# Reads as plain float32 products, and products of zeros where the planner expects TensorE to wait

## The chip, the cores and the metric

The program runs on one core of a Trainium2 chip, in one launch. The metric is the device time of that launch in microseconds (us). The profile names five engines: PE is TensorE (PEld its weight loads), DVE is VectorE, ACT is ScalarE, POOL is GpSimd, and SP issues most transfers.

## What is computed

Three stages follow each other; the second needs all rows of the first, since its rows are sorted by expert.

```python
def _attn_ref(x, state):                     # x 8x8x512x64, state 8x8x32x64
    scores = scale * np.matmul(x, state.transpose(0, 1, 3, 2))
    a = softmax(scores)                      # over the 32 states
    xread = np.matmul(a, state)
    scores2 = scale * np.matmul(state, x.transpose(0, 1, 3, 2))
    a2 = softmax(scores2)                    # over the 512 tokens
    sread = np.matmul(a2, x)
    return np.concatenate([xread, sread], axis=2)

def _moe_ref(x, expert_emb, tau, w1, w2):    # 4352 rows of 512, 8 experts
    expert_idx = np.argmax(xn @ en.T / tau, axis=1)
    out[mask] = gate_w[mask, None] * (np.maximum(x[mask] @ w1[e], 0.0) @ w2[e])

def _moe2_ref(x, w_in, w_out):               # 512 to 2048 to 512
    h = x @ w_in
    return (h * np.clip(h + 3.0, 0.0, 6.0) / 6.0) @ w_out
```

(`softmax` stands for the lines with max, exp and sum; the reads of the title are `xread`.)

## The kernel before

**Stages.** The attention works batch by batch (eight batches of 544 rows). `o_X` transposes the tokens on PE, `o_sc` forms the scores, `o_scs` to `o_nm` make the two softmaxes on DVE, ACT and POOL, `o_aT` transposes the weights of the first one back, and `o_xr` multiplies them by the states: four reads `xr` a batch, each of two halves. The states stand in a masked form, `sd`, which POOL makes for each batch (`o_sd`), with eight more columns that give the router's logits. `o_xrc` copies the read out of PSUM and `o_xd` stores it in DRAM (`xd`). In the last two batches the logits are taken by `o_lg` on DVE. Then `o_top`, `o_scan`, `o_rk`, `o_rank`, `o_bt`, `o_at`, `o_pg` and `o_gidx` sort the rows by expert: `rk` and `pg` are short products on PE, and `gidx` holds the row numbers that POOL gathers by.

**Float32 in two parts.** A product with an operand of type float32r is done from parts: the rounded value and what is left of it (`ah`, `al`; `sdh`, `sdl`; `wh`, `wl`), as high by high, high by low and low by high. ACT or DVE makes the high part, DVE or POOL the low part. The attention's transposes and scores are plain float32 products instead, without parts.

**The expert layer.** The first five slots of 128 rows belong to the largest expert (the lead: `QUAD` of four slots and `FIFTH`); POOL gathers them into `xg`, ACT or DVE reorders them (`xp`), PE transposes them (`m_g`), and `L1w`/`L1` and `L2` form `h_g` and `y_g`. After the lead come eleven pairs of slots and ten single slots (`h_ps`, `y_ps`). Four further single slots stand in nested conditions at the program's end, which the run of the profile does not enter. Weights come in 512 KB loads (`raw`), of which two buffers exist; `load_w` makes `wh` and `wl`.

**The feed-forward layer** works on blocks of 256 rows: `F1` (tile `u_ps`, 12 products for each of 16 pieces) and `F2` (tile `o`, 6 products). Its weights are stored in a packed form, and `convert` unpacks each of the 32 pieces in eight steps on ACT, DVE and POOL (`cv_raw`, `cv_m`, `wih`, `wil`, `woh`, `wol`); eight of these fall into the attention. `F1` and `F2` stand between the pairs and singles.

**What sets the order.** Each engine works through its instructions strictly in the order in which they are written. That order comes from a planner (`Sched`): every step has a priority, an engine or a choice of engines (`"*"` in `BY`), and an assumed cost. `run` takes the step that can begin soonest, weighed with its priority, and advances the assumed clocks. PSUM and SBUF buffers are rings that a step takes and gives. So a changed cost can move steps on every engine, up to the point where the orders agree again: on PE that is the region of the fourth pair (about 440 us in the trace); behind it PE's order is the old one.

`REST` and `COLD` let the planner charge a slow start after an idle time of PE. `o_warm` runs 14 products at the very beginning.

Of the kernel before, what the change touches and what calls it, by code (L numbers as in the profile page):

```python
# [8 lines left out]
F32 = mybir.dt.float32  # L9
# [29 lines left out]
class Sched:  # L39
# [60 lines left out]
    def run(self, until=None):  # L100
        while self.avail and not (until and until()):
# [53 lines left out]
def kernel(  # L155
# [60 lines left out]
    def quarters(t, g):  # L216
# [28 lines left out]

    NRAW, NW, NROW, NGX = 2, 3, 6, 4
# [3 lines left out]
        ps=4, ax=NAX, xT=NXT, scs=NSC, e2=NE2, e1=NE1, a2=NA2, ah=NAH, al=NAH, xr=NXR, sd=2, sx=1, xs=1, acr=2,  # L250
# [110 lines left out]
    def ps(name):  # L361
        return pa.tile([128, 2, 512], F32, tag="ps", name=name)
# [84 lines left out]
    gh_ = one.tile([128, B, 2, E], F32R, name="gh_")  # L447
    gl_ = one.tile([128, B, 2, E], F32R, name="gl_")
    sth = one.tile([128, B, 2, D], F32R, name="sth")
    stl = one.tile([128, B, 2, D], F32R, name="stl")  # L450
# [31 lines left out]
    def o_sth(b0, b1):  # L482
        ACT.copy(sth[:, b0:b1], st[:, b0:b1])

    def o_stl(b0, b1):
        bs = slice(b0, b1)
        DVE.tensor_tensor(stl[:, bs], st[:, bs], f32(sth[:, bs]), op=ALU.subtract)
# [32 lines left out]
    def o_warm():  # L520
        p = ps("warm")
        for _ in range(14):
            PE.matmul(p[:, 0, 0:128], ident, ident, start=True, stop=True)

    def o_sd(b):
        res = []
        for s_, g_, nm in ((sth, gh_, "sdh"), (stl, gl_, "sdl")):
            t = ap2.tile([128, 2, W // 2], F32R, tag=nm, name=nm)
            for g in range(2):
                v = t[:, g].rearrange("p (h q w) -> p h q w", h=2, q=2)  # L530
                for h in range(2):
                    POOL.tensor_tensor(
                        v[:, h, :, 0:64].rearrange("p q (i a) -> p q i a", i=2),
                        f32(s_[:, b, g, :]).rearrange("p (q a) -> p q a", q=2).unsqueeze(2).to_broadcast([128, 2, 2, 32]),
                        bmask.rearrange("p (i h) -> p h i", i=2)[:, h].unsqueeze(1).unsqueeze(3).to_broadcast([128, 2, 2, 32]),
                        op=ALU.mult)
            POOL.tensor_copy(t.rearrange("p g (q w) -> p g q w", q=4)[:, :, :, 64:66],
                             f32(g_[:, b]).rearrange("p g (q i) -> p g q i", q=4))
            res.append(t)
        V["sd", b] = res  # L540
# [124 lines left out]
    def o_ah(b, r0, r1):  # L665
        if r0 == 0:
            V["ah", b] = ap1.tile([128, 2, 512], F32R, tag="ah", name="ah", bufs=NAH)
        k = slice(r0 * 128, r1 * 128)
        ACT.copy(V["ah", b][:, :, k], V["aT", b, r0][:, :, k])

    def o_al(b, r0, r1):
        if r0 == 0:
            V["al", b] = ap1.tile([128, 2, 512], F32R, tag="al", name="al", bufs=NAH)
        k = slice(r0 * 128, r1 * 128)
        DVE.tensor_tensor(V["al", b][:, :, k], V.pop(("aT", b, r0))[:, :, k], f32(V["ah", b][:, :, k]), op=ALU.subtract)

    def parts(b):
        ah, al = V["ah", b], V["al", b]
        sh, sl = V["sd", b]
        return (ah, sh), (ah, sl), (al, sh)  # L680

    def o_xr(b, r):
# [82 lines left out]
    def group(b0, b1, prio):  # L765
# [11 lines left out]
        q2 = op(lambda: o_gp(b0, b1), {"D": 0.35}, prio + 2, [q1])  # L777
        s1 = op(lambda: o_sth(b0, b1), {"A": 0.22 + 0.13 * n}, prio + 2, [ld], (), [hst])
        s2 = op(lambda: o_stl(b0, b1), {"D": 0.06 + 0.14 * n}, prio + 2, [s1], (), [hst])
        for b in range(b0, b1):  # L780
            st_ready[b], g_ready[b] = c, [q2, s2]
# [12 lines left out]
        X0c='A', X1c='*', nm='P', a2c='A', x0c='*', x1c='*', x2c='A', x3c='*', q1='A')  # L794

    PARTS = [(0, R)], [(k, k + R // 2) for k in (0, R // 2)]
    def batch(b, t, last):
# [3 lines left out]
        bscs, be2, ba2, bah, bal, bxr, bsd = (hold(n) for n in ("scs", "e2", "a2", "ah", "al", "ax" if last else "xr", "sd"))  # L801
# [40 lines left out]
        sd = do("sd", o_sd, {"P": 3.2}, g_ready[b], [bsd], port="P")  # L842
        for (r0, r1), scs in zip(chunks, scs_):
# [1060 lines left out]
```

## Time and profile before

| what | us |
|---|---|
| median of 3 runs | 1457.59 (1456.26 to 1458.63) |
| the profiled execution, its own time | 1456.29 |
| its span in the trace | 1454.6 |
| PE busy, DVE busy | 1349.5, 917.5 |
| ACT busy, POOL busy | 598.0, 433.8 |

Busy times are sums of an engine's own instructions and overlap between engines. A matrix product is recorded from its start to its modelled end, some 0.17 us after the next can begin, so distances between starts tell what a product costs in a row of them. PEclk is the TensorE clock that was granted, as a share of 2.4 GHz; 0.5 is its lower level, 1.2 GHz. Row L1650 and the like are lines of the kernel before.

### The profile page before, as it was taken

The numbers are of one execution on the slowest core, as the hardware profiler recorded it, in microseconds if no ns is written. First come the engines' busy times: TensorE is split into PE (matmuls) and PEld (weight loads), VectorE is DVE, ScalarE is ACT, GpSimd is POOL, SyncE is SP. The second block draws the span as 40 slices with busy tenths as digits, with TensorE's granted clock in tenths as the row PEclk, the third lists the DMA queues.
The fourth block names the chain that finished last, engine by engine and source line by source line (L and its number), as shares of the span: only waits on it lengthen the run. The fifth ranks groups of instructions, "written<-read, shape, count | busy, mean of one in ns | idle before, by whom it ended". The sixth has DMA issues, their size and how long they took to land. (4 is left out here: it accounts for less than half of the span.)

```text
span 1454.6 us, 25083 instructions
## 1 busy us (share of the span) xinstructions
PE 1349.5 (93%) x8976; PEld 1195.2 (82%) x8976; DVE 917.5 (63%) x2108; ACT 598.0 (41%) x1290; POOL 433.8 (30%) x483
## 2 busy tenths in 40 slices
PE   7985698787789999999999999999999999999997
PEld 5765676677678898988899898998988999899996
DVE  6988777688766545655564645777867676434332
ACT  3775425455434333424333343343344444333332
POOL 5453427414143242325132133332423311100000
PEclk8998689898899999999999999999999999999999
DMA  6654326556465333334333232545554544101000
GB/s 160 169 168 141 121 70 179 156 172 190 136 190 168 95 103 105 111 92 120 119 97 114 91 117 88 173 145 159 172 153 145 163 151 141 57 23 30 16 15 15
DMA packets 151765, 175.63 MB, mean 121 GB/s; under 512 B 43785, under 2 KB 116489, under 8 KB 150609
## 3 DMA queue, kind: packets, MB, share of 16 engines
q1 hardware_dynamic: 128544, 121.19, 27.7%
q0 software_dynamic: 12336, 35.99, 8.1%
q10 hardware_dynamic: 10752, 16.78, 3.7%
q8 instruction: 73, 1.20, 0.4%
q14 instruction: 60, 0.48, 0.1%
HBM read 146.09 MB, written 27.82 MB: 120 GB/s over the span
## 5 line engine op out<-in xcount | busy, mean ns | idle before, releaser
L1650 PE MATMUL u_ps<-yh,wih 128*128 128x256 f32 x1088 | 306.5, 282 | 9.0 <-ACT yh L1626 8.1
L1650 PE MATMUL u_ps<-yw,wih 128*128 128x256 f32 x1088 | 306.5, 282 | 0.1
L1650 PE MATMUL u_ps<-yh,wil 128*128 128x256 f32 x1088 | 306.0, 281 | 0.0
L1654 ACT ACTIVATE r<-u_ps,three 128x256 f32<-128x256 f32 x272 | 129.2, 475 | 353.0 <-PE u_ps L1650 348.5
L1657 DVE SCALAR_TENSOR_TENSOR u_ps<-r,u_ps 128x256 f32<-128x256 f32 x272 | 116.4, 428 | 226.1 <-ACT r L1654 225.5
L1650 PEld LDWEIGHTS u_ps<-yh,wih 128*128 128x128 f32 x1088 | 206.7, 190 | 18.3 <-ACT yh L1626 8.3
L1685 PE MATMUL o<-woh,gh 128*128 128x512 f32 x544 | 217.0, 399 | 1.5 <-DVE yo L1699 1.2
L1685 PE MATMUL o<-wol,gh 128*128 128x512 f32 x544 | 216.1, 397 | 0.0
L1685 PE MATMUL o<-woh,gl 128*128 128x512 f32 x544 | 214.8, 395 | 0.0
L1650 PEld LDWEIGHTS u_ps<-yw,wih 128*128 128x128 f32 x1088 | 206.0, 189 | 8.5 <-DVE yw L1629 0.4
L1650 PEld LDWEIGHTS u_ps<-yh,wil 128*128 128x128 f32 x1088 | 206.6, 190 | 0.0
L1280 DVE TENSOR_TENSOR wl<-raw,wh 128x512 fp32r<-128x512 f32 x275 | 192.9, 711 | 11.3 <-ACT wh L1277 6.9
L1544 PE MATMUL y_ps<-wh,hx 128*128 128x512 f32 x512 | 185.7, 399 | 0.0
L1661 ACT CAST gh<-u_ps 128x256 fp32r<-128x256 f32 x272 | 101.4, 373 | 201.9 <-PE o L1685 162.3
L1664 DVE TENSOR_TENSOR gl<-u_ps,gh 128x256 fp32r<-128x256 f32 x272 | 114.8, 422 | 108.2 <-ACT gh L1661 107.6
L1280 POOL TENSOR_TENSOR wl<-raw,wh 128x512 fp32r<-128x512 f32 x77 | 105.3, 1368 | 245.9 <-DVE wh L1277 124.7
L1308 POOL DMA_INDIRECT xq<-xd,qidx x128 | 131.8, 1030 | 85.0 <-DVE xt L1361 34.1
L1441 PE MATMUL h_ps<-xt,wh 128*128 128x256 f32 x704 | 141.3, 290 | 1.4 <-DVE wh L1277 1.0
L1277 DVE CAST wh<-raw 128x512 fp32r<-128x512 f32 x223 | 96.4, 436 | 64.2 <-DMA raw<-in_moe_w_dram 29.4
L1704 POOL DMA_INDIRECT out_dram<-yo,ix x34 | 37.8, 1112 | 320.1 <-DVE yo L1699 219.1
L1685 PEld LDWEIGHTS o<-woh,gl 128*128 128x128 f32 x544 | 102.4, 188 | 25.1
L1441 PEld LDWEIGHTS h_ps<-xt,wh 128*128 128x128 f32 x704 | 118.1, 198 | 4.1 <-PE u_ps L1650 1.2
(307 smaller groups left out, 2342.3 us busy)
## 6 DMA issues: line engine op xcount, KB each, us to landing
raw<-in_moe_w_dram SPq DMA_DIRECT2D x176, 512.0 KB, 4.0
yl<-ysd SPq DMA_DIRECT2D x136, 64.0 KB, 2.4
xd<-xr SPq DMA_DIRECT2D x8, 1056.0 KB, 4.5
ysd<-yt POOLq DMA_DIRECT2D x32, 256.5 KB, 3.3
xb<-in_x_dram SPq DMA_DIRECT2D x48, 128.0 KB, 2.9
yw<-in_moe_w_out_dram ACTq DMA_DIRECT2D x9, 512.0 KB, 4.5
cv_raw<-in_moe_w_in_dram ACTq DMA_DIRECT2D x8, 512.0 KB, 4.6
yh<-in_moe_w_in_dram ACTq DMA_DIRECT2D x8, 512.0 KB, 4.6
```

The lines of the kernel that those rows point to most:

```text
L1277: copy[e](pc["hi"], box["t"][:, j, :])
L1280: eng[e].tensor_tensor(pc["lo"], box["t"][:, j, :], f32(pc["hi"]), op=ALU.subtract)
L1308: POOL.indirect_dma_start(q[:, j * QW:(j + 1) * QW], None, xd_q, index(qidx[:, j, s:s + 1]))
L1441: PE.matmul(out(f), pc[w][:, (2 * c + f) * 128:(2 * c + f + 1) * 128], u.xt[a][:, 2 * j + c, 256 * hf:256 * hf + 256], start=new and c == ...
L1544: PE.matmul(u.y[i], u.ht[t][:, a, lo + 128 * i:lo + 128 * i + 128], pc[w], start=c == 0 and k == 0, stop=c == KF - 1 and k == 2)
L1650: PE.matmul(p, w, y[:, k, :], start=k == 0 and j == 0, stop=k == KD - 1 and j == 2)
L1654: ACT.activation(q["r"], q["p"], AF.Relu, bias=pool["three"][:, 0:1])
L1657: DVE.scalar_tensor_tensor(q["p"], q["r"], 6.0, q["p"], op0=ALU.min, op1=ALU.mult)
L1661: ACT.copy(q["h"], q["p"])
L1664: DVE.tensor_tensor(q["l"], q["p"], f32(q["h"]), op=ALU.subtract)
L1685: PE.matmul(o["o"][a], g[:, a * 128:(a + 1) * 128], w, start=m == 0 and j == 0, stop=m == KFF - 1 and j == 2)
L1704: POOL.indirect_dma_start(out, bass.IndirectOffsetOnAxis(ap=o["ix"][:, a:a + 1], axis=0), box["t"], None)
```

## The change

It has two parts.

**Reads as plain float32 products.** The parts of the read go: `o_gp`, `o_stl`, `o_al` and the second half of `o_sd` (the tile `sdl`) are dropped, `ah`, `sd` and the copied state `stk` are plain float32, and a read takes two products of 264 columns where it took six. The copy `ah` may now go to ACT or to DVE (the planner puts the last half batch's second half on DVE, all others on ACT), the read's assumed cost goes from 0.66 to 0.9, that of `o_sd` from 3.2 to 1.65.

**Products of zeros.** When the planner lets PE begin a step later than its clock, the difference is kept in `gap`. The function `busy`, called when a step has its PSUM tile and before its own products, writes `int((gap - 0.5) / 0.055)` products of 128 columns, at most 160, if the gap is over 1.0. Both operands are `none`: the low halves of the identity's float32 values, read as bfloat16 (every second element), which are zero. Where a tile is already in use they add zero to it. `o_warm` gets 70 of these as well.

```diff
+            self.gap = b - self.clk["T"] if e == "T" else 0.0
             o.fn(e) if len(o.cost) > 1 else o.fn()
...
+    none = ident.bitcast(BF16).rearrange("p (c t) -> p c t", t=2)[:, :, 0]
+
+    def busy(p, start=True):
+        gap, sc.gap = sc.gap, 0.0
+        n = min(int((gap - 0.5) / 0.055), 160) if gap > 1.0 else 0
+        for _ in range(n):
+            PE.matmul(p[:, 0:128], none, none, start=start, stop=start)
...
     def ps(name):
-        return pa.tile([128, 2, 512], F32, tag="ps", name=name)
+        p = pa.tile([128, 2, 512], F32, tag="ps", name=name)
+        busy(p[:, 0, :])
+        return p
...
-    def o_gp(b0, b1):
-        bs = slice(b0, b1)
-        DVE.tensor_copy(gh_[:, bs], gq[:, bs])
-        DVE.tensor_tensor(gl_[:, bs], gq[:, bs], f32(gh_[:, bs]), op=ALU.subtract)
...
-    def o_al(b, r0, r1):
...
-        DVE.tensor_tensor(V["al", b][:, :, k], V.pop(("aT", b, r0))[:, :, k], f32(V["ah", b][:, :, k]), op=ALU.subtract)
...
+        for _ in range(70):
+            PE.matmul(p[:, 0, 0:128], none, none, start=True, stop=True)
...
         for g in range(2):
-            for i, (a, s) in enumerate(parts(b)):
-                PE.matmul(p[:, g, 0:256 + E], a[:, g, r * 128:(r + 1) * 128], s[:, g, :], start=i == 0, stop=i == 2)
+            PE.matmul(p[:, g, 0:256 + E], V["ah", b][:, g, r * 128:(r + 1) * 128], V["sd", b][:, g, :], start=True, stop=True)
...
-        X0c='A', X1c='*', nm='P', a2c='A', x0c='*', x1c='*', x2c='A', x3c='*', q1='A')
+        X0c='A', X1c='*', ah='*', nm='P', a2c='A', x0c='*', x1c='*', x2c='A', x3c='*', q1='A')
...
-        sd = do("sd", o_sd, {"P": 3.2}, g_ready[b], [bsd], port="P")
+        sd = do("sd", o_sd, {"P": 1.65}, g_ready[b], [bsd], port="P")
...
-            a = do("xr", o_xr, {"T": 0.66}, deps[r], [hp] + ([bxr] if r == 0 else []), [bah, bal, bsd], args=(r,),
+            a = do("xr", o_xr, {"T": 0.9}, deps[r], [hp] + ([bxr] if r == 0 else []), [bah, bsd], args=(r,),
...
+            busy(u.hp[q][0][:, 0:256], False)
```

(The other calls of `busy`, in `o_pg`, `ptile`, `L1`, `L2`, `F1` and `F2`, are of the same kind.)

**Where the zeros stand** in the changed program: 70 behind `warm`; 18 ahead of the first state transposes; 10 ahead of the second batch's token transposes; at the end of the attention 27 ahead of a `sr`, 17 ahead of `sx`, 38 ahead of the last `a_ps`, 39 ahead of the second `rk` and 56 ahead of `pg_ps`; in the lead 87, 29, 29 and 22 ahead of `m_g` transposes, 13 ahead of the first `h_g` and 55 ahead of the last 30 `y_g`; in the pairs 26, 68, 9, 32, 58 and 65 ahead of `h_ps` and 89 ahead of `y_ps` products. That makes 857 in 20 places. No zeros stand behind the fourth pair but for those in the conditional slots.

At the end of the attention, on DVE, the last logits (`lg`) and the first steps of the sort stood like this before; `cv_m` are steps of a weight conversion:

```order
L699 COPY lg<-xr_ps 128x8
L700 TENSOR_TENSOR lg<-lg,xr_ps 128x8
L303 TENSOR_SCALAR cv_m<-cv_raw 128x512
L304 SCALAR_TENSOR_TENSOR cv_m<-cv_raw,cv_m 128x512
L308 SCALAR_TENSOR_TENSOR cv_m<-cv_raw,cv_m 128x512
L316 SCALAR_TENSOR_TENSOR cv_m<-cv_raw,cv_m 128x512
L699 COPY lg<-xr_ps 128x8
L700 TENSOR_TENSOR lg<-lg,xr_ps 128x8
L962 TENSOR_REDUCE mx_1883<-lg 128x9
```

On the same engine, in the same place of the changed program (where `L687` and `L688` are the logits and `L947` begins the sort):

```order
L687 COPY lg<-xr_ps 128x8
L688 TENSOR_TENSOR lg<-lg,xr_ps 128x8
L947 TENSOR_REDUCE mx_1853<-lg 128x9
L949 TENSOR_TENSOR cand_1855<-lg,mx_1853 128x72
L950 SCALAR_TENSOR_TENSOR cand_1855<-cand_1855,iota_e 128x72
L952 TENSOR_REDUCE exp<-cand_1855 128x9
```

The four conversion steps no longer stand between the last two logits; they were moved ahead of them or behind the sort.

At the start of the lead, on POOL, the five gathers stood like this before (`wil` is a step of a weight conversion, `nr` of the gates, `wl` the low part of an expert weight):

```order
L327 TENSOR_TENSOR wil<-cv_m,wih 128x512 x2
L1302 DMA xg<-xd,gidx_78 128x528 x5
L1378 TENSOR_TENSOR nr<-nr,half 128x1 x2
L327 TENSOR_TENSOR wil<-cv_m,wih 128x512
L1378 TENSOR_TENSOR nr<-nr,half 128x1
L1280 TENSOR_TENSOR wl<-raw,wh 128x512
```

On the same engine, in the same place of the changed program:

```order
L339 TENSOR_TENSOR wil<-cv_m,wih 128x512
L1288 DMA xg<-xd,gidx_78 128x528 x2
L339 TENSOR_TENSOR wil<-cv_m,wih 128x512
L1288 DMA xg<-xd,gidx_78 128x528 x3
L1364 TENSOR_TENSOR nr<-nr,half 128x1 x2
L339 TENSOR_TENSOR wil<-cv_m,wih 128x512
L1364 TENSOR_TENSOR nr<-nr,half 128x1 x2
L1266 TENSOR_TENSOR wl<-raw,wh 128x512
```

A conversion step now stands between the second and the third gather, and the first low parts of the expert's weights come from here (DVE made the first two before). On PE the change puts all five transposes `m_g` ahead of the first `h_g`, where before 24 products `h_g` stood among them; and in the first pair, all 96 products `h_ps` stand ahead of the first `u_ps`, where it was 72.

## Rows read from the trace of the kernel before

**Rows 1.** The page: the granted clock of PE in 40 slices, tenths.

```profile
PEclk8998689898899999999999999999999999999999
```

**Rows 2.** Stretches: us, each engine's busy time (instructions), granted clock, DMA, GB/s.

```profile
0.00:22.00 22.00, 15.09 (x72) 11.74 (x72) 12.18 (x31) 4.12 (x7) 14.26 (x35) 0.77 0.73 191
22.00:110.00 88.00, 77.22 (x990) 59.76 (x989) 77.10 (x151) 62.62 (x102) 38.06 (x76) 1.00 0.55 161
110.00:151.00 41.00, 22.74 (x212) 19.90 (x210) 32.63 (x96) 19.83 (x34) 12.41 (x18) 0.78 0.37 128
151.00:247.00 96.00, 80.94 (x430) 67.72 (x431) 75.60 (x198) 43.52 (x97) 48.74 (x46) 0.83 0.39 118
247.00:443.00 196.00, 154.75 (x887) 136.44 (x886) 148.51 (x326) 94.85 (x195) 62.05 (x61) 0.90 0.57 172
443.00:1454.60 1011.60, 998.76 (x6394) 899.65 (x6392) 571.53 (x1311) 373.02 (x856) 258.30 (x249) 1.00 0.35 106
```

**Rows 3.** Groups of 0 to 151 us: busy us, mean ns, idle before.

```profile
L675 DVE TENSOR_TENSOR al<-a_ps,ah 128x1024 fp32r<-128x1024 f32 x7 | 8.6, 1223 | 0.5 <-ACT ah L669 0.3
L692 DVE COPY xr<-xr_ps 128x528 f32<-128x528 f32 x5 | 3.5, 692 | 1.0 <-PE xr_ps L689 0.5 <-issue 0.4
```

**Rows 4.** PE in time, one batch: start us, us, instruction, records.

```profile
79.75 1.94 PE L560 MATMUL sc_ps<-xT,stT 128*64 128x512 f32 x8
...
84.03 0.28 PE L689 MATMUL xr_ps<-sdl,ah 128*128 128x264 f32 x1
...
85.98 0.28 PE L689 MATMUL xr_ps<-sdh,al 128*128 128x264 f32 x1
```

**Rows 5.** PE in time, the start; in brackets idle before and releaser.

```profile
1.48 6.00 PE L523 MATMUL warm<-ident 128*128 128x128 f32 x28 [1.48 <-POOL ident masks.py:199]
12.23 0.59 PE L442 MATMUL enT_ps<-ident,em 8*128 8x8 f32 x4 [4.76 <-DVE em L439]
...
14.65 3.68 PE L547 MATMUL xT_ps<-ident,xb 128*128 128x128 f32 x16
18.26 3.09 PE L560 MATMUL sc_ps<-xT,stT 128*64 128x512 f32 x8
```

**Rows 6.** DVE in time, the end of the attention.

```profile
138.78 0.43 DVE L303 TENSOR_SCALAR cv_m<-cv_raw 128x512 int32<-128x512 int32 x1
...
141.44 0.16 DVE L699 COPY lg<-xr_ps 128x8 f32<-128x8 f32 x1
...
150.83 0.17 DVE L1103 SCALAR_TENSOR_TENSOR gidx<-pg_ps,gj 128x5 int32<-128x5 f32 x1
```

**Rows 7.** PE in time, from the sort to the lead.

```profile
144.65 0.25 PE L981 MATMUL rk_ps<-hsum,ones 128*128 128x80 bf16 x1 [6.09 <-DVE hsum L977]
...
156.13 1.11 PE L1334 MATMUL m_g<-ident,xp 128*128 128x128 f32 x4 [5.54 <-ACT xp L1329]
...
183.69 0.60 PE L1504 MATMUL t_ps<-ident,hs 128*128 128x128 f32 x4
```

**Rows 8.** POOL in time, the fifth gather, and the conversion step behind it.

```profile
157.87 1.01 POOL L1302 DMA_INDIRECT xg<-xd,gidx  x1 [0.30 <-issue]
...
159.99 1.26 POOL L327 TENSOR_TENSOR wil<-cv_m,wih 128x512 fp32r<-128x512 f32 x1
```

**Rows 9.** PE's bfloat16 products: one line in time, one group.

```profile
211.95 0.32 PE L1115 MATMUL q_g<-pj,sel 128*128 128x82 bf16 x4
...
L1097 PE MATMUL pg_g<-at,bts 128*128 128x164 bf16 x34 | 10.2, 473 | 0.0
```

**Rows 10.** PE in time, waits in the lead and the pairs.

```profile
238.21 0.50 PE L1544 MATMUL y_g<-wl,hx 128*128 128x512 f32 x1 [3.48 <-DVE wl L1280]
...
270.11 0.58 PE L1650 MATMUL u_ps<-yh,wih 128*128 128x256 f32 x1 [8.05 <-ACT yh L1626]
```

**Rows 11.** Stretches: the last `y_g`, and some pairs (columns as Rows 2).

```profile
216.00:247.00 31.00, 27.52 (x116) 21.86 (x115) 25.58 (x56) 18.32 (x39) 25.85 (x25) 0.94 0.59 170
...
319.40:352.00 32.60, 21.01 (x116) 18.58 (x115) 30.14 (x62) 22.43 (x46) 16.28 (x15) 0.84 0.42 131
```

More of the change, by code (lines that the diff above doesn't have):

```diff
@@ L53, in __init__ @@
         self.wp, self.port, self.cold = 0.0, 0.0, 0.0
-        self.avail, self.n = [], 0
+        self.avail, self.n, self.gap = [], 0, 0.0
     def op(self, fn, cost, prio, deps=(), take=(), give=(), dma=0.0, after=None, port=""):
@@ L446 @@
     gq = one.tile([128, B, 2, E], F32, name="gq")
[L447 to L450, printed above, removed]
+    stk = one.tile([128, B, 2, D], F32, name="stk")
     V = {}
@@ L475, in o_gqc, with o_stk @@
         ACT.copy(gq[:, b0:b1], V["gq", b0][:, 0, 0:(b1 - b0) * 2 * E].rearrange("p (b g e) -> p b g e", g=2, e=E))
-    def o_gp(b0, b1):
-        bs = slice(b0, b1)
-        DVE.tensor_copy(gh_[:, bs], gq[:, bs])
-        DVE.tensor_tensor(gl_[:, bs], gq[:, bs], f32(gh_[:, bs]), op=ALU.subtract)
[L482 to L487, printed above, removed]
+    def o_stk(b0, b1):
+        ACT.copy(stk[:, b0:b1], st[:, b0:b1])
     def flat(p):
@@ L523, in o_warm @@
             PE.matmul(p[:, 0, 0:128], ident, ident, start=True, stop=True)
+        for _ in range(70):
+            PE.matmul(p[:, 0, 0:128], none, none, start=True, stop=True)
     def o_sd(b):
[L526 to L540, printed above, removed]
+        t = V["sd", b] = ap2.tile([128, 2, W // 2], F32, tag="sd", name="sd")
+        for g in range(2):
+            v = t[:, g].rearrange("p (h q w) -> p h q w", h=2, q=2)
+            for h in range(2):
+                POOL.tensor_tensor(
+                    v[:, h, :, 0:64].rearrange("p q (i a) -> p q i a", i=2),
+                    stk[:, b, g, :].rearrange("p (q a) -> p q a", q=2).unsqueeze(2).to_broadcast([128, 2, 2, 32]),
+                    bmask.rearrange("p (i h) -> p h i", i=2)[:, h].unsqueeze(1).unsqueeze(3).to_broadcast([128, 2, 2, 32]),
+                    op=ALU.mult)
+        POOL.tensor_copy(t.rearrange("p g (q w) -> p g q w", q=4)[:, :, :, 64:66],
+                         gq[:, b].rearrange("p g (q i) -> p g q i", q=4))
     def o_X(b, v, r0, r1):
@@ L663, in o_aT, with o_ah @@
                 PE.transpose(p[:, g, r * 128:(r + 1) * 128], an[:, k:k + 128], ident)
-    def o_ah(b, r0, r1):
+    def o_ah(e, b, r0, r1):
         if r0 == 0:
-            V["ah", b] = ap1.tile([128, 2, 512], F32R, tag="ah", name="ah", bufs=NAH)
+            V["ah", b] = ap1.tile([128, 2, 512], F32, tag="ah", name="ah", bufs=NAH)
         k = slice(r0 * 128, r1 * 128)
-        ACT.copy(V["ah", b][:, :, k], V["aT", b, r0][:, :, k])
-    def o_al(b, r0, r1):
-        if r0 == 0:
-            V["al", b] = ap1.tile([128, 2, 512], F32R, tag="al", name="al", bufs=NAH)
-        k = slice(r0 * 128, r1 * 128)
-        DVE.tensor_tensor(V["al", b][:, :, k], V.pop(("aT", b, r0))[:, :, k], f32(V["ah", b][:, :, k]), op=ALU.subtract)
[L677 to L680, printed above, removed]
+        copy[e](V["ah", b][:, :, k], V.pop(("aT", b, r0))[:, :, k])
     def o_xr(b, r):
@@ L800, in batch @@
         hsc, ha2, hsr = (hold("ps") for _ in range(3))
-        bscs, be2, ba2, bah, bal, bxr, bsd = (hold(n) for n in ("scs", "e2", "a2", "ah", "al", "ax" if last else "xr", "sd"))
+        bscs, be2, ba2, bah, bxr, bsd = (hold(n) for n in ("scs", "e2", "a2", "ah", "ax" if last else "xr", "sd"))
         def do(name, f, cost, *a, args=(), late=0.0, **k):
@@ L1094, in o_pg @@
         p = pool["g_ps"].tile([128, 512], F32, tag="g", name="pg_g") if i else ps("pg_ps")[:, 0, :]
+        busy(p)
         p = V["pg", i] = p[:, 0:k * n].rearrange("p (a s) -> p a s", a=k)
@@ L1416, in ptile @@
     def ptile(u, name):
-        return pool["g_ps"].tile([128, 512], F32, tag="g", name=name + "_g") if u.lead else \
+        p = pool["g_ps"].tile([128, 512], F32, tag="g", name=name + "_g") if u.lead else \
             pool["pm"].tile([128, 512], F32, tag="m", name=name + "_ps")
+        busy(p)
+        return p
     PARTS3 = ((0, "hi"), (0, "lo"), (1, "hi"))
@@ L1479, in mm @@
                 u.hp[v] = ptile(u, "h")
+            busy(u.hp[v][:, 0:256], False)
             for c in range(2):
@@ L1541, in mm @@
                         u.y[i] = y[:, i, :]
+                    busy(u.y[0])
+            busy(u.y[ii[0]], False)
             for i in ii:
@@ L1645, in mm @@
             p = q["p"] = pool["pu"].tile([128, 256], F32, tag="u", name="u_ps")
+            busy(p)
             yh, yw = o["y"]
@@ L1681, in mm @@
                 o["o"] = [pool["po"].tile([128, DM], F32, tag=f"o{a}", name=f"o{a}") for a in range(2)]
+            busy(o["o"][0], not m)
             woh, wol = (w[:, m % (KFF // 2), :] for w in wo_t[m // (KFF // 2)])
```

13 lines of the change are left out of this document (5 added, 8 removed).

## The prediction, made before the changed kernel ran

> **What bounds the kernel now.** I read the clock in slices first, then the busy times by stretch, then PE in time wherever the clock is low, and last DVE and POOL in time at the steps PE waits for.
>
> The slices [rows 1] show the full clock everywhere but in the first slice and in slices 4 to 11. The table by stretch [rows 2] says what lies there. From 443 us on PE is busy 998.76 of 1011.60 us at 1.00. The change leaves that part's order alone, so every microsecond by which PE arrives there earlier counts once, and nothing can be gained behind it. Ahead of it PE is not the only bound: from 22 to 110 us PE (77.22) and DVE (77.10 of 88) are level, from 110 to 151 DVE leads with 32.63 of 41 while PE has 22.74, and from 151 to 443 PE is busy 235.7 of 292 us beside a DVE with 224.1. The waits are PE's: 4.76 us at the start [rows 5], 6.09 and 5.54 around the sort [rows 7], 3.48 and 8.05 in lead and pairs [rows 10].
>
> The granted clock follows those waits. There are two levels, so a mean of 0.78 is the lower one for (1 − 0.78)/0.5 = 44% of a stretch. That makes 10 us at 1.2 GHz up to 22 us, 18 us from 110 to 151, 33 us from 151 to 247, and 39 us from 247 to 443 [rows 2]. Work done in that time takes up to twice as long. With PE busy for 69%, 55%, 84% and 79% of those stretches, at most half of 7 + 10 + 28 + 31 = 76 us, so **38 us**, could come back from a clock that never falls. The zeros can reach only part of it: they stand in 20 places and do nothing for the waits of DVE and DMA themselves.
>
> The profiled run took 1456.29 us, 1.69 more than its span of 1454.6, and the median is 1.3 above it; I sum against 1456.29 and add 1.3.
>
> **The reads.** On PE: in each of the 4 × 2 halves that a batch reads, three float32r products of 264 columns become one of plain float32. The old price is (85.98 − 84.03)/16 = 0.122 us from start to start [rows 4], so 0.366 a half. A plain float32 product of 264 columns is not in the trace. The nearest row is `sc`: four plain float32 products of 512 columns in 1.94 us, run two side by side on one half of the array each (the row's 128*64). Less the 0.17 of a modelled end that is 1.77/2 = 0.885 us for 512 columns, and 264/512 × 0.885 = 0.45 us. If they ran one after the other it would be 0.23. That is 8 × (0.45 − 0.366) = +0.7 us a batch, or 8 × (0.23 − 0.366) = −1.1; over eight batches +5 or −9 of PE time. I take +5, since the half-array shape stands in the row itself.
>
> On DVE: `al` goes, seven of 1.22 us, and two halves of the last batch at some 0.7, 10.0 us [rows 3]. The `gh_`, `gl_` and `stl` steps go with it, about 3.8 us by the sizes of such rows. DVE takes on two copies of token transposes, two more `xr` copies and half an `ah`, some 4.3 us at 0.69 a piece and up [rows 3]. So DVE is relieved of about 9.3 us, nearly all of it before 138 us. ACT loses 4 us of copies; POOL loses half of `sd`, some 13 us, which lie beside other work (38 of 88 us busy [rows 2]) and which I cost at nothing. From 22 to 110 us PE and DVE are level, so with DVE 9 us lighter and PE 5 us heavier, PE becomes the bound. What can be gained is the time that PE waits there, 88 − 77.2 = 10.8 us, less the 5 added; a pipeline of many short steps never fills it whole, and I take **−2.5** (0 to −6).
>
> At the end of the attention DVE did four conversion steps between two last logits, from 138.78 to 141.44 us [rows 6], and the sort begins only behind them. In the new order they stand elsewhere: −2.7. The last half batch also loses an `al` between `ah` and the read, −0.5, and gets no later otherwise, since PE is done at about 138.5 (144.65 less 6.09) [rows 7]. Together **−3**. What was moved must be done somewhere: ahead of it DVE has the time that `al` gave up; were it missing there, this term would be about −0.5.
>
> **The zeros, where they help.** At the start 70 stand behind `warm`, which ends at 7.5 us, while PE idles until 12.23 [rows 5]. Token transposes took 3.68 us for 16 and the first scores 3.09; at full clock the rows of [rows 4] give the scores in 1.94, and 16 transposes in half of 3.68 or little less. That would be −1.1 and up to −1.9, so −3; the 18 zeros ahead of the first state transposes have no wait before them here and cost 1.1 at 60 ns, so **−2**.
>
> In the lead the fifth gather begins at 157.87, and the conversion step that now stands ahead of it on POOL costs 1.26 [rows 8]. All five transposes now come before the first `h_g`. From `gidx` (151.0 [rows 6]) to the last of 132 `h_g` products (183.69 [rows 7]) it took 32.7 us. Now: fifth gather issued at 6.9 + 1.3 = 8.2 after `gidx`; from the issue of the first gather (151.98) to its transpose (156.13 [rows 7]) some 4.2, and with the steps of five slots queued on ACT and DVE I take 8, so `h_g` begins 16 after `gidx`; 132 × 0.12 = 15.9 at full clock. That is 32 against 32.7: **−1**, between −4 (no queue) and +3 (clock still low). Thus most of what the clock gives there is given back by waiting for the fifth slot. The last `y_g` stand behind 55 zeros: the clock is 0.94 from 216 to 247 [rows 11], so 3.7 us at the lower level, worth 1.8 at most, **−1.5**.
>
> In the pairs 24 more `h_ps` are put into the 8.05 us ahead of the first `u_ps` [rows 10], 24 × 0.12 = 2.9, and the clock stays up behind it. Of the 39 us at the lower level, most lies where DVE sets the pace: from 319.4 to 352 DVE is busy 30.14 of 32.60 us at a clock of 0.84 [rows 11], and a faster PE waits longer there. So of the 15 us bound for this stretch I take 2.9 + 1.6 = **−4.5** (0 to −10).
>
> **The zeros, where they cost.** A zero product's price is not in the trace. Four products `q_g` of 82 columns, bfloat16 too, take 0.32 us, one 0.205, so 38 ns from start to start; for 128 columns 60 ns [rows 9]. The change reckons 55 and leaves 0.5 us, so 60 ns overruns the foreseen wait only in runs of over 100, of which there is none. But foreseen waits are not real ones. Where rows show the wait, the zeros fit at 60 ns: 39 (2.3 us) into the 6.09 ahead of the second `rk`, 87 (5.2) into the 5.54 ahead of the first `m_g` [rows 7], 55 (3.3) into 3.48, and 68 (4.1) with 24 `h_ps` (2.9) into 8.05 [rows 10]. For the other runs, whose waits move with the order, I add **+1.5** in all, 0.1 a run. The other row of bfloat16 products speaks for a dearer one: `pg_g`, 34 products of 164 columns in 10.2 us, 299 ns each [rows 9], read 34 elements apart, so 1.8 ns a column. `none` is read 2 elements apart, and its 128 columns would cost 230 ns at that rate. I take 60, because a step of two elements keeps to the 4 bytes that a float32 column also takes, and 264 of those pass in 122 ns [rows 4].
>
> The Trainium skill ("TensorE: Matmul & The Clock Gate", section "Back-to-back issue gap") gives about 81 ns for a product of 128 columns in a stream of weight loads and products, against 56 for an isolated one, and so speaks against this change. `q_g`, scaled, is nearer to the second, but only four stand in a row there, so no row here settles it; by the 81 the time would be close to that of rival 2.
>
> **Sum.** −2 (start) −2.5 (reads) −3 (end of the attention) −1 (fifth gather) −1.5 (`y_g`) −4.5 (pairs) +1.5 (overruns) = −13.0: span 1441.6, run 1443.3, median 1444.6, rounded to **1445**.
>
> **Rivals.** 1. *Only the reads' gain arrives.* The zeros hold the clock, but PE then waits for DVE, transfers or the fifth gather: the level DVE [rows 2, 11] and the gather's delay [rows 8] speak for it; against it, that lead and pairs each hold over 25 us of PE work at the lower clock [rows 2]. What is left is −3 at the attention's end and −1 of the rest: 1457.6 − 4 = **1453.6**.
>
> 2. *Zeros are dearer, but not ruinous.* Less than half of the way from 60 ns to rival 3's 118, at 83, a run of n zeros overruns its foreseen wait by 0.028 n − 0.5, which over all runs comes to 14.1 us; the other terms make −14.5, and the gain is gone: **1457.6** at most, a little less by the slack of real waits. For it: long runs of such short products are not in the trace. Against it: `xr`'s 264 columns keep to their 0.122 us over 16 in a row [rows 4].
>
> 3. *Slower: the products of zeros do not keep the clock up.* Then they run at 1.2 GHz, 118 ns each (twice 59), and 857 of them overrun by 0.063 n − 0.5, about 43 us, less 15 where real waits are longer than foreseen, with only 6 of the gain left: some **1480**. In the same way a strided read of 230 ns gives 0.175 n − 0.5, about 140 us, less some 12 of slack: 1585. It decides from about 83 ns a product on. For it: no row shows products of zeros at all, and during `pg_g`, whose products fill PE without a break [rows 9], the clock is not full in the surrounding stretch (0.83 [rows 2]). Against it: 28 records of `warm` [rows 5] are small products as well, and the clock is at 1.00 soon after small ones throughout 22 to 110.
>
> **How the numbers follow.** Forecast 0.64, rival 1 0.17, rival 2 0.06, rival 3 0.09, and 0.04 for a gain beyond the range, if the pairs give back over 10. The range takes in the low ends (−2.5 to −6 for the reads, −4.5 to −8 in the pairs, −1 to −4 in the lead: 1435) and rival 1 with the overruns (1456). A difference of 0.2%, 2.9 us, is about what a measurement of this kernel can tell from no change. Faster: the forecast, the larger gain and most of rival 1, 0.80; within 0.2%: the rest of it and rival 2, 0.09; slower: rival 3 and the dear end of rival 2, 0.11.
>
> **What would show it.** In the trace of the changed kernel: zeros 55 to 60 ns apart (118 or more: rival 3); a clock of 0.9 and over from 110 to 443, PE at 1.00 behind `warm`; the plain read at about 0.44 from start to start; no `cv_m` between the last two logits, and `gidx` at about 143.5 (−2 −2.5 −3); the last `h_g` 32 us after `gidx`; PE dense at full clock from about 430. If `gidx` is early but that point is not, rival 1 holds. The forecast is wrong if a run of zeros stands on the path with its data already there, or if the reads cost PE more than DVE saves.

## The result, and the profile after

The changed kernel takes **1445.7 us** (median of 4 runs, 1443.71 to 1445.98) where the kernel before, run beside it, takes 1458.1. The ratio is 0.9908, with a 95% interval of 0.9885 to 0.9930: faster by about 0.9%. The forecast was 1445, with a range of 1435 to 1456. Total and range held; of the steps behind them only a part did, as the experiments below show.

The profiled execution took 1445.98 us, its span is 1444.3, 10.3 less than before. The same stretches as in [rows 2], in the changed kernel:

```profile
0.00:22.00 22.00, 17.74 (x172) 14.78 (x172) 12.73 (x32) 5.34 (x11) 12.68 (x30) 1.00 0.79 192
22.00:110.00 88.00, 81.90 (x992) 63.34 (x991) 74.27 (x155) 64.17 (x108) 31.64 (x48) 1.00 0.56 162
110.00:151.00 41.00, 35.60 (x448) 32.35 (x447) 31.03 (x104) 18.52 (x34) 13.69 (x18) 0.92 0.49 164
151.00:247.00 96.00, 87.95 (x598) 75.71 (x596) 73.26 (x183) 40.50 (x92) 50.17 (x47) 0.91 0.44 125
247.00:443.00 196.00, 172.59 (x1233) 153.39 (x1233) 154.90 (x334) 92.27 (x195) 64.67 (x62) 0.95 0.56 170
```

The granted clock rose in every stretch where it had been below 1.00: 0.77 to 1.00 at the start, 0.78 to 0.92, 0.83 to 0.91 and 0.90 to 0.95. That the products of zeros did this, and not the new order, the first experiment shows. (PE's busy time includes the zeros.) The start, PE in time, against [rows 5]:

```profile
6.44 4.17 PE L527 MATMUL warm<-ident 128*128 128x128 bf16 x70
12.25 0.41 PE L456 MATMUL enT_ps<-ident,em 8*128 8x8 f32 x4 [1.64 <-DVE em L453]
12.60 1.21 PE L255 MATMUL stT_ps<-ident 128*128 128x128 bf16 x18
...
15.04 1.97 PE L547 MATMUL xT_ps<-ident,xb 128*128 128x128 f32 x16
```

Seventy zeros take 4.17 us, less the modelled end 4.0, so **57 ns** each; the 16 token transposes fell from 3.68 to 1.97 us. At the end of the attention and in the sort, against [rows 7]:

```profile
124.94 3.75 PE L255 MATMUL a_ps<-ident 128*128 128x128 bf16 x38 [2.52 <-DVE lg L688]
128.53 0.60 PE L663 MATMUL a_ps<-ident,e 128*128 128x128 f32 x4
128.97 3.73 PE L677 MATMUL xr_ps<-sd,ah 128*128 128x264 f32 x16
132.53 2.40 PE L255 MATMUL rk_ps<-ident 128*128 128x128 bf16 x39
135.65 0.20 PE L966 MATMUL rk_ps<-hsum,ones 128*128 128x80 bf16 x1 [0.71 <-DVE hsum L962]
```

Eight plain float32 products (two records each) take 3.73 us, less the modelled end 0.445 us for 264 columns. The reads end at 132.70 us, before at 138.56; the second `rk` begins at 135.65 instead of 144.65. But the first row also shows zeros at work where nothing has to be bridged: PE waited 2.52 us for a PSUM tile, and then did 38 zeros, 3.75 us at mostly half clock, ahead of transposes whose weights POOL had finished at 122.54. The lead, against [rows 7] and [rows 8]:

```profile
150.87 1.82 PE L255 MATMUL m_g<-ident 128*128 128x128 bf16 x29
154.00 0.75 PE L1320 MATMUL m_g<-ident,xp 128*128 128x128 f32 x4 [1.30 <-ACT xp L1315]
...
155.85 2.55 PE L255 MATMUL m_g<-ident 128*128 128x128 bf16 x22
158.20 0.86 PE L1320 MATMUL m_g<-ident,xp 128*128 128x128 f32 x4
...
175.46 0.60 PE L1494 MATMUL t_ps<-ident,hs 128*128 128x128 f32 x4
```

The 22 zeros in 2.55 us show the price at the lower clock, some 107 ns. `gidx` is done at 141.91 and the first `t_ps` begins at 175.46: 33.55 us, where it was 32.7.

The rest of this text follows the kernels along six points of PE's order: the last read, `gidx`, the first `t_ps` (all 132 `h_g` are done), the last `y_g`, the 601st record of `u_ps` (behind all places where the orders differ), and the span's end. Before and after, by stage, from the timelines, in us:

| stage | before | after | difference | forecast |
|---|---|---|---|---|
| to the last read | 138.56 | 132.70 | −5.9 | −5.0 |
| to `gidx` | 12.43 | 9.21 | −3.2 | −2.7 |
| to the first `t_ps` | 32.70 | 33.55 | +0.9 | −1 |
| to the last `y_g` | 63.09 | 61.05 | −2.0 | −1.5 |
| to the 601st `u_ps` | 333.90 | 333.92 | 0.0 | −4.5 |
| to PE's end | 865.66 | 865.85 | +0.2 | 0 |

Each kernel was traced once per job, and the same stage of the same program differs between traces. The changed kernel was traced a second time (e9, below): to the last read and to `gidx` the two agree within 0.2 us, but behind the 601st `u_ps` it takes 868.5 us instead of 865.9. Differences of a few us in one stage of one pair of traces are therefore no proof.

### The profile page after: what moved, and what is told of

It is laid out like the page before. It is cut to its first block, busy times and chain, and to the rows that moved or that the text cites. A ratio compares the mean times of both kernels' runs of the same rounds, so it can differ in the third digit from the quotient of the medians.

```text
span 1444.3 us, 26620 instructions
## 1 busy us (share of the span) xinstructions
PE 1384.4 (96%) x9769; PEld 1230.8 (85%) x9769; DVE 906.9 (63%) x2102; ACT 588.3 (41%) x1276; POOL 425.0 (29%) x445
## 5 line engine op out<-in xcount | busy, mean ns | idle before, releaser
L1643 PEld LDWEIGHTS u_ps<-yh,wih 128*128 128x128 f32 x1088 | 205.7, 189 | 12.4 <-DVE gl L1657 3.8
L1266 POOL TENSOR_TENSOR wl<-raw,wh 128x512 fp32r<-128x512 f32 x80 | 111.3, 1393 | 250.8 <-DVE wh L1263 122.4
L1263 DVE CAST wh<-raw 128x512 fp32r<-128x512 f32 x232 | 101.5, 440 | 63.1 <-PE y_ps L1536 23.2
```

The source lines that it names most:

```text
L1263: copy[e](pc["hi"], box["t"][:, j, :])
L1266: eng[e].tensor_tensor(pc["lo"], box["t"][:, j, :], f32(pc["hi"]), op=ALU.subtract)
L1643: PE.matmul(p, w, y[:, k, :], start=k == 0 and j == 0, stop=k == KD - 1 and j == 2)
```

## The experiments

All times are medians in us; ratios are against the kernel before in the same job, with 95% intervals.

**No zeros at all (e1).** Two edits in the changed kernel:

```diff
-        n = min(int((gap - 0.5) / 0.055), 160) if gap > 1.0 else 0
+        n = 0
...
-        for _ in range(70):
-            PE.matmul(p[:, 0, 0:128], none, none, start=True, stop=True)
```

> The changed kernel without any product of zeros (neither the 70 behind `warm` nor the 787 others); all other instructions stand in the same order on every engine. As the prediction summed it, the zeros bring 2 at the start, 1.5 at the last y_g, some 1.6 of the 4.5 in the pairs, and what the clock does for the h_g of the lead (some 3), and cost 1.5 in overruns: without them 1445.7 + 6.6, about 1452. Rival, the time comes from the plain reads and the new order alone: 1444 to 1447. Rival, it comes from the zeros alone: 1456 or more.

Measured: **1445.95**, ratio 0.9922 (0.9902 to 0.9941). The first rival holds: plain reads and the new order alone give what the whole change gives. Its clock is the old one:

```profile
110.00:151.00 41.00, 22.60 (x183) 18.13 (x184) 31.67 (x102) 18.82 (x35) 13.46 (x17) 0.74 0.46 158
151.00:247.00 96.00, 82.50 (x450) 69.27 (x451) 74.96 (x188) 40.80 (x91) 47.78 (x48) 0.84 0.45 126
247.00:443.00 196.00, 163.59 (x924) 144.94 (x923) 154.64 (x336) 93.48 (x196) 63.91 (x63) 0.90 0.57 171
```

So the zeros raised the clock from 0.74 to 0.92, from 0.84 to 0.91 and from 0.90 to 0.95, and the time did not change by more than the intervals allow (0.9922 against 0.9908; the changed kernel again, in e9, 0.9927). By stage, the zeros (changed kernel less this one) bring −0.9 to the last read, −0.1 to `gidx`, −0.6 to the first `t_ps`, −1.0 to the last `y_g`, and cost +3.9 in the pairs; behind them −1.3.

**Zeros alone (e2).** The kernel before with `gap`, `busy` and its calls as in the change, and the 70 behind `warm`; reads and order as before:

```diff
+            self.gap = b - self.clk["T"] if e == "T" else 0.0
...
+        for _ in range(70):
+            PE.matmul(p[:, 0, 0:128], none, none, start=True, stop=True)
```

> The kernel before, its reads in three float32r products and its order unchanged, with the products of zeros added by the same rule (70 behind `warm`, 798 in 21 other places before the fourth pair). By the prediction's terms: 2 at the start, 1.5 at the last y_g, 1.6 in the pairs, some 3 for the h_g, less 1.5: 1458.1 - 6.6, about 1451.5. Rival, only the reads and the order matter: 1457 to 1459. Rival, zeros that run over with their data already there cost more than the clock gives back: 1460 or more.

Measured: **1453.1**, ratio 0.9967 (0.9953 to 0.9980), near the forecast's own terms. In its trace the gain is made in the lead (from `gidx` to the last `y_g` 91.0 us, before 95.8), and half of it is lost in the pairs (336.2 to the 601st `u_ps`, before 333.9). In the lead the zeros thus bring 4.8 us in the old order, where `h_g` stand between the transposes, and 1.5 in the new one, where all `h_g` wait for the fifth slot. That this wait is the reason fits the traces, but no run shows it.

**No zeros in the pairs (e3).** `n` is set to 0 from the 14th run on:

```diff
+        if n:
+            i = len(ZN)
+            ZN.append(n)
+            n = n if i < 13 else 0
```

> The changed kernel with its zeros up to the last y_g, and none of the 347 in the pairs; the order is the same. The prediction gave the clock 1.6 us there: about 1447.3. Rival, read from the two traces: the last y_g ends 10.3 us earlier (246.78 and 236.51) and the whole span is 10.3 us shorter, PE waits for wl behind nearly every run of zeros in the pairs, so weights set the pace there and the zeros bring nothing: 1445.7, within 1 us. Rival, the zeros hold PE up there: 1443 or less.

Measured: **1443.9**, ratio 0.9907 (0.9888 to 0.9926). Not slower, so the forecast's net gain from zeros in the pairs isn't there; whether they do harm is seen in e11.

**Fewer zeros (e4).** Five runs that stand before ready data are left out (`n = 0 if i in (0, 1, 2, 4, 11) else n`, by the same counter).

> The changed kernel without five runs of zeros that stand before products whose data was there in its trace: the 18 ahead of the first state transposes, 10 ahead of the second batch's token transposes, 27 ahead of an sr, 38 ahead of the last a_ps (3.75 us at half clock, its weights done 2.4 us before the first zero) and 13 ahead of the first h_g. If they stood on the path: -1 for the 18, -3.7 for the 38, -0.7 for the 13, so about 1440.5. Rival, another chain (DVE's, or the gathers') ends as late: 1444 to 1446. Rival, the clock falls where the 38 are gone and the last reads and the sort pay for it: 1446 or more.

Measured: **1449.0**, ratio 0.9948 (0.9928 to 0.9968), in the range of the third theory alone, but not for its reason. (The changed kernel measured 1449.3 itself in e9, so it isn't certain that e4 is slower.) In its trace the last `y_g` ends at 232.13 us, 4.4 earlier than in the changed kernel, near the first theory. But e6, the same program up to there, has it at 234.26, and the program with all five, at 236.51 in the changed kernel, has it at 235.63 in e9 and 233.56 in e3. So what the five runs cost lies between nothing and 4 us. In e4's trace some 2 us of the lead went in the pairs, and the rest and more at one place that was not in any theory. PE in time at 1071 us, first the changed kernel, then this one, each with the row of its stretch:

```profile
1073.60 0.38 PE L1472 MATMUL h_ps<-wh,xs 128*128 128x256 f32 x1 [0.76 <-DVE wh L1263]
1075.10 0.39 PE L1472 MATMUL h_ps<-wl,xs 128*128 128x256 f32 x1 [1.11 <-POOL wl L1266]
1075.32 0.40 PE L1472 MATMUL h_ps<-wh,xs 128*128 128x256 f32 x2
...
1060.00:1090.00 30.00, 28.13 (x190) 25.31 (x189) 19.52 (x46) 11.09 (x25) 9.12 (x9) 1.00 0.57 179
```

```profile
1073.37 0.38 PE L1478 MATMUL h_ps<-wh,xs 128*128 128x256 f32 x1 [2.37 <-DVE wh L1269]
1074.87 0.58 PE L1478 MATMUL h_ps<-wl,xs 128*128 128x256 f32 x1 [1.11 <-POOL wl L1272]
1075.25 0.63 PE L1478 MATMUL h_ps<-wh,xs 128*128 128x256 f32 x2
...
1060.00:1090.00 30.00, 26.52 (x161) 23.97 (x160) 16.39 (x39) 9.83 (x22) 8.97 (x9) 0.89 0.47 139
```

The weights come at almost the same time, 1073.6 and 1073.4. The earlier PE waits 2.37 us instead of 0.76, the clock falls (the same pair of products takes 0.63 instead of 0.40), and by the 2051st `u_ps` it is 2.3 us behind the kernel that came later.

**Zeros at the late wait (e6).** The kernel of e4 with 38 zeros ahead of that one step, the 43rd `L1` step of a single slot:

```diff
+            if not u.lead:
+                LZ.append(k)
+                if len(LZ) == 43:
+                    for _ in range(38):
+                        PE.matmul(u.hp[v][:, 256 * (q % 2):256 * (q % 2) + 128], none, none, start=j == 0, stop=j == 0)
```

> e4_fewer_zeros with 38 products of zeros ahead of one h_ps step of a single slot, at about 1071 us, where its trace has PE wait 2.37 us for wh and then 1.11 for wl, with a granted clock of 0.89 from 1060 to 1090 us (1.00 in the changed kernel, whose wait there is 0.76). If the fall of the clock behind that wait is what costs e4 its lead of 2 us: about 2.3 less than e4, 1446.5. Rival, the weights come when they come and the clock matters nothing: 1449 as e4.

Measured: **1444.9**, ratio 0.9923 (0.9895 to 0.9951), 4 us less than e4 (the intervals of the two ratios overlap). Its clock from 1060 to 1090 us is 1.00 again:

```profile
1060.00:1090.00 30.00, 29.30 (x223) 26.71 (x222) 19.41 (x46) 11.40 (x25) 9.91 (x11) 1.00 0.45 141
```

It crosses 1071 us with 1.3 us lost where e4 lost 3.3 (distance to the kernel before, 1801st to 2001st `u_ps`: −14.1 to −12.8, against −11.2 to −7.9). So 2 us at this place hang on the zeros; some of the 4 us lies in the pairs, where the two kernels are the same and still differ by 4.6. All traces together say the same of the clock, and less of the wait. From the 1801st to the 2051st `u_ps` the six whose clock fell there lose 2.0 to 4.5 us against the kernel before (e1, e2, e3, e4, e5, e8), the six whose clock stayed up 0.4 to 2.1 (after, e9 and, with zeros there, e6, e7, e10, e11). But the length of the wait for `wh` doesn't decide it alone: the clock fell behind 0.58 (e2), 1.11 (e8) and 1.17 us (e1) as well, each with 1.11 for `wl` behind it, and stayed up behind 1.31 and 1.11 (e9).

**The reads alone (e5).** The kernel before in its own order, with plain reads; `o_gp`, `o_stl` and `o_al` issue nothing, but the planner still reckons with them:

```diff
     def o_al(b, r0, r1):
-        if r0 == 0:
-            V["al", b] = ap1.tile([128, 2, 512], F32R, tag="al", name="al", bufs=NAH)
-        k = slice(r0 * 128, r1 * 128)
-        DVE.tensor_tensor(V["al", b][:, :, k], V.pop(("aT", b, r0))[:, :, k], f32(V["ah", b][:, :, k]), op=ALU.subtract)
+        V.pop(("aT", b, r0))
...
-            for i, (a, s) in enumerate(parts(b)):
-                PE.matmul(p[:, g, 0:256 + E], a[:, g, r * 128:(r + 1) * 128], s[:, g, :], start=i == 0, stop=i == 2)
+            PE.matmul(p[:, g, 0:256 + E], V["ah", b][:, g, r * 128:(r + 1) * 128], V["sd", b][:, g, :], start=True, stop=True)
```

> The kernel before with its order unchanged on every engine, and of the change only the plain float32 reads: the two parts, al, gh_, stl and the second half of sd are not issued, but the planner still reckons with them. No zeros. By the prediction's terms the reads bring 2.5 and the last al 0.5, the rest (four conversion steps moved, lead, pairs) needs the new order: 1458.1 - 3, about 1455. Rival, the reads themselves bring nearly all of the 12 us that the changed kernel gains without zeros: 1446 to 1449. Rival, PE's 5 us more are on the path: 1459 or more.

**The reads with `al` kept (e8).** As e5, but `o_al` still subtracts, into a tile that no product reads.

> As e5_reads_alone, but DVE still issues al (9 steps, 10.0 us) into a tile that nobody reads, so it no longer stands between ah and the reads. If DVE's time is what the reads give back: as slow as before plus PE's 5, 1457 to 1460. If the wait for al ahead of the reads is what counts: as e5.

Measured: **1452.7**, ratio 0.9970 (0.9951 to 0.9988), and **1455.2**, ratio 0.9990 (0.9972 to 1.0008): e5 lies between its theories, e8 below its first one, nearer to it than to its second. Their intervals overlap; the traces part them more clearly. The end of the attention, PE in time, e5 and then e8:

```profile
138.29 0.25 PE L962 MATMUL rk_ps<-hsum,ones 128*128 128x80 bf16 x1 [5.94 <-DVE hsum L958]
```

```profile
144.08 0.25 PE L965 MATMUL rk_ps<-hsum,ones 128*128 128x80 bf16 x1 [5.96 <-DVE hsum L961]
...
L665 DVE TENSOR_TENSOR al<-a_ps,ah 128x1024 fp32r<-128x1024 f32 x7 | 8.6, 1223 | 0.5 <-ACT ah L659 0.3
L665 DVE TENSOR_TENSOR al<-a_ps,ah 128x512 fp32r<-128x512 f32 x2 | 1.4, 692 | 1.0 <-ACT ah L659 1.0
```

The reads alone bring the second `rk` from 144.65 to 138.29, 6.4 us; with `al` done but off the reads' path it is 144.08, 0.6 us. So what the reads give back comes with leaving out `al`, 10 us of DVE's time, not with the wait for it ahead of the reads, and not from PE, which does 5 us more in both. (In e8 `al` also still reads the PSUM tile `a_ps`, so that this tile comes free as late as before; no run parts this from DVE's time.) Where e5 gains, its row from 22 to 110 us shows against [rows 2]:

```profile
22.00:110.00 88.00, 83.00 (x972) 62.51 (x970) 70.23 (x147) 66.01 (x111) 30.92 (x52) 1.00 0.55 162
```

PE is busy 83.00 us instead of 77.22, DVE 70.23 instead of 77.10, and the fifth batch's last read ends at 94.22 us instead of 98.53. So 4.3 of the 6.2 us that e5 has gained at the last read (132.35 instead of 138.56) are there by then. Behind the attention e5 keeps 7.6 us up to the 1801st `u_ps` and then loses 3.0 at the place of e4, with a clock of 0.94 from 1060 to 1090 us.

**Fitted zeros (e7; e9 to e11).** By the same counter, zeros only where the changed kernel's trace has PE wait without data: 17, 39, 56, 72 (for 87), 29, 29, 14 (for 22) and 55 besides the 70 behind `warm`, 40 at the late wait, none in the pairs.

```diff
+            n = {3: 17, 5: 39, 6: 56, 7: 72, 8: 29, 9: 29, 10: 14, 12: 55}.get(i, 0)
```

> The changed kernel with zeros only where its trace has PE wait with no data there: 70 behind `warm`, 17, 39, 56, 72 (for 87), 29, 29, 14 (for 22), 55, then 40 at the late wait of e6_zeros_at_late_wait, and none in the pairs. If what e3 and e4 gained up to 600 us (2 to 5 us) adds up and is kept behind 1071 us: 1441. Rival, the weights set the pace behind the lead and give it back: 1444 to 1446. Rival, less zeros in the pairs and more waiting behind it: over 1446.

Measured: **1439.7**, ratio 0.9889 (0.9866 to 0.9912). It was run again beside the changed kernel, and beside a third that differs from it only in the pairs' 347 zeros, which are put back:

> The changed kernel once more, as the base of comparison for the two beside it: 1444 to 1447.

> e7_fitted_zeros once more, beside the changed kernel: if its gain stands, 4 to 6 us less than the changed kernel, 1439 to 1442. Rival, the difference was one of chips: within 2 us of it.

> e7_fitted_zeros with the 347 zeros in the pairs put back, where the planner put them. If weights set the pace there and zeros only get in the way (from the last y_g to the 600th u_ps product it took 331 to 336 us with them in the new order, 328 to 332 without): 3 to 4 us slower than e10. Rival, they do neither good nor harm: as e10. As the prediction had it, 1.6 us faster than e10.

Measured: the changed kernel **1449.3** (0.9927, 0.9906 to 0.9949), above its expectation; the fitted one **1441.9** (0.9883, 0.9865 to 0.9902); with the pairs' zeros **1445.0** (0.9906, 0.9889 to 0.9922). The fitted kernel beats the changed one by 7 us here, of which 3 lie in the zeros of the pairs: the first theory of e11 holds. Their runs, side by side, don't overlap (e10 at most 1444.30, e11 at least 1444.36). The traces of e7 and then e11, from the last `y_g` (233.72 and 233.65 us) to the 601st `u_ps`, each with PE's waits for DVE's `wl` (us in all, times, longest):

```profile
233.72:561.77 328.05, 288.92 (x1753) 258.60 (x1752) 230.44 (x520) 141.90 (x308) 109.67 (x109) 0.94 0.49 152
...
PE h_ps L1436 <- DVE wl L1272: 20.6, 6, 5.7
PE y_ps L1549 <- DVE wl L1272: 7.2, 2, 6.7
```

```profile
233.65:569.25 335.60, 309.25 (x2100) 277.13 (x2100) 230.92 (x520) 142.58 (x308) 109.57 (x109) 0.95 0.50 148
...
PE h_ps L1436 <- DVE wl L1272: 8.4, 6, 3.5
PE y_ps L1549 <- DVE wl L1272: 2.1, 5, 0.8
```

With zeros PE is busier by 20.3 us and waits less, but not less by as much; DVE does the same work in both. Over all traces with the new order it takes from the last `y_g` to the 601st `u_ps` 333.9, 335.4, 335.9, 331.2 and 335.6 us with zeros in the pairs (after, e9, e4, e6, e11), and 330.0, 332.2, 328.1 and 331.8 without (e1, e3, e7, e10): 334.4 against 330.5 on average. The same program differs by up to 4.6 us there and the two groups touch, so a single pair of traces would settle nothing; the nine, with the runs of e10 and e11, speak for some 3 to 4 us.

The nine also show how. The 347 zeros take 19.8 us (57 ns each), and PE's waits fall by 11.3, from 38.3 to 27.1 us on average, so 8.5 us of zeros stand where PE did not wait. The other products take 4.7 us less, 288.4 instead of 293.0, at a clock of 0.96 instead of 0.94. That leaves the 3.9. In all five traces, behind all seven runs of zeros, the next product starts without a wait (of 0.15 us or more); in 23 of these 35 cases a wait follows within the seven products behind that one, most often for `wl`.

A single place can mislead. With the 68 zeros PE begins the first product with `wl` behind them 2.7 us later than without (e7, then e11, PE and DVE in time):

```profile
254.03 0.58 PE L1436 MATMUL h_ps<-xt,wl 128*128 128x256 f32 x1 [3.87 <-DVE wl L1272]
...
253.29 0.68 DVE L1272 TENSOR_TENSOR wl<-raw,wh 128x512 fp32r<-128x512 f32 x1
```

```profile
252.27 4.07 PE L261 MATMUL h_ps<-ident 128*128 128x128 bf16 x68
256.75 0.38 PE L1436 MATMUL h_ps<-xt,wl 128*128 128x256 f32 x1 [0.24 <-DVE wl L1272]
...
256.01 0.69 DVE L1272 TENSOR_TENSOR wl<-raw,wh 128x512 fp32r<-128x512 f32 x1
```

But it is not these zeros that hold it up: it still waits 0.24 us for `wl`, which DVE itself makes 2.7 us later in that trace.

## Why the prediction was right, and where only its sum was

**Bound: right up to 443 us, too simple behind it.** That PE is dense from 443 us on held, but not that each microsecond of arrival counts once. At 1071 us the weights of a single slot set the pace: [rows 2] show 998.76 of 1011.60 us busy, and one wait for weights in the remaining 13, with the clock that falls in or behind it, takes back 3 us from e3, e4 and e5. In its first trace the changed kernel was spared: its distance to the kernel before is −10.3 at the 601st `u_ps` and −10.1 at the end. That was luck of this trace: in its second one (e9) it goes from −9.6 to −6.8, and the trace of every other kernel loses 1.1 to 5.2 us behind the 601st `u_ps`.

**Price of a zero: right.** 57 ns at full clock against 60 forecast, 107 at the lower one against 118; the read two elements apart adds nothing to the 60 that were forecast without it. This settles the rule of the Trainium skill ("TensorE: Matmul & The Clock Gate", section "Back-to-back issue gap") for these products: some 81 ns for streams of weight loads and products is too much here, where 70 in a row, each with its own weight load, keep to 57. Rivals 2 and 3 fell with it.

**Start: right.** The first `sr` begins at 23.94 us instead of 26.07, −2.1 (forecast −2). Without any zeros it is 25.8. The price of the 18, 1.1, isn't shown: without them it is 23.1 in e4, but 24.4 to 24.7 in the four other traces that leave them out.

**Reads on PE: right, on DVE: half of the true size.** The read costs 0.445 us, forecast 0.45 from the scores' row. But of DVE's relief I let only 2.5 us arrive, with 0.5 for the last half batch; e5 shows 6.2 at the last read, and e8, in which DVE keeps `al`, 0.4. The step that failed is the size in "a pipeline of many short steps never fills it whole, and I take −2.5": with 5 us more to do, PE's idle time from 22 to 110 us fell from 10.8 to 5.0, and 4.3 us were gained by the fifth batch's read (1.1 of them before the first `sr`). Another 1.9 came in the three batches behind it, for which I had reckoned 0.5. In the changed kernel only −5.9 shows at that point, start included. One reason is in its order: from the last read of the fifth batch to that of the sixth it takes 17.3 us in every trace of the new order, with zeros or without, before 14.9; by which step isn't shown. The zeros ahead of ready data took back less: five traces without them reach the last read at 130.1 to 132.0 us (e4, e6, e7, e10, e11), three with them at 131.3 to 132.9 (after, e3, e9), 1.0 later on average.

**End of the attention: right.** From the last read to `gidx` 9.21 us instead of 12.43; the four conversion steps were worth 3, forecast 2.7. e1 shows the same without zeros, so it is the order.

**Fifth gather: inside its bounds, wrong side.** I took −1, between −4 and +3; measured +0.9. The first `h_g` comes 17.7 us after `gidx`, not 16, and then the 132 take 15.85 as reckoned. Without the zeros that stand there too long it is 16.6 (e4) and 16.3 (e7).

**Last `y_g`: right.** −1.5 from the first `y_g` to the last (33.87 to 32.35 us).

**Pairs: wrong.** −4.5 was forecast, 0.0 came. Without zeros the new order takes 330.5 us on average of four traces; the old order, also without zeros, takes 333.9, 332.2 and 330.3 (before, e5, e8). So the 24 `h_ps` moved ahead of the `u_ps` gain some 1.6 of my 2.9, if that, since the traces scatter by as much. The step that failed is "the zeros fit at 60 ns", with an overrun of 0.1 us a run for all others. The price was right and the clock even gave more than my 1.6 (4.7 us), but 8.5 us of the zeros stood where PE did not wait. I had held each run against a wait of the planner or of the old trace; in the new order the product behind each run started at once, and the wait, where one followed, was for the `wl` of the products after it. I had read that DVE sets the pace there (30.14 of 32.60 us [rows 11]).

**Sum.** By stage the attention with the sort brought 1.4 us more than forecast, the last `y_g` 0.5 more, the gather 1.9 less and the pairs 4.5 less, and the 1.5 for overruns is in these stages. So the profiled runs differ by 10.3 us against a forecast of 13.0; the medians, which the forecast was made for, differ by 12.4, and by 9.7 when measured again (e9). That the total came within 1 us is luck: terms wrong by 1 to 5 us, in both directions, met in it. And the prediction's own sign of being wrong, "a run of zeros stands on the path with its data already there", did show, in the pairs. Rival 1, to which I gave 0.17, has the mechanism better than my forecast: only the reads and the order's gain arrive. It had the wrong size (4 us instead of 12), in part from the same term that I had mis-sized. What e1 shows is that the zeros of this change are worth nothing on balance. Placed by the trace they are worth some 5 us (ratios 0.9889 and 0.9883 in e7 and e10 against 0.9922 in e1; these were other jobs).

Open is what each single run of zeros costs or gives; the runs in the pairs were put back all together. Open is also why the same clock stays up behind one wait at 1071 us and falls behind a shorter one.

## What to carry to other kernels

An idle engine can be kept at its clock by work without effect, but such work stands in an in-order queue: place it by the waits of a trace of the same order, not by those a planner foresees. Where another engine sets the pace, set what the clock can give back against the part of the filler that won't fit into a wait; in the pairs here that was 4.7 us against 8.5. When an edit relieves one engine and loads another, a guess at how much of the relief arrives is the weakest term; a run that leaves the order alone measures it (e5, e8). Before a stage's difference is explained, trace the same kernel twice. And a total that comes out as forecast proves none of its terms: only leaving out one half of the change (e1, e2) showed which of them was there.

## What the hardware showed that was not expected

Products of zeros, each with its own weight load, hold the granted clock up: 1.00 up to 22 us against 0.77 without, 0.92 from 110 to 151 us against 0.74 without (e1). Read two elements apart, 128 of their bfloat16 columns take 57 ns, where 164 columns of `pg_g`, read 34 apart, take 299 ns [rows 9]; that the step is the reason was not varied by itself.

And arriving earlier can cost time. At 1071 us a wait of 0.76 and then 1.11 us left the clock at full speed, 2.37 and 1.11 us did not, and the kernel that came 1.8 us earlier was 2.3 us behind soon after. It isn't a matter of the longer wait alone: 0.58 and 1.11 us let the clock fall in e2, 1.31 and 1.11 didn't in e9.
